# An eighth place for x in the column loop of a Hyena and MoE kernel, and three rooms instead of four for VectorE's weighted rows

## The chip, the cores and the metric

The kernel runs on one core of one Trainium2 chip. The metric is the device time of one execution in microseconds (us), as the median of several runs. Five engines work side by side: TensorE (PE, with its weight loads as PEld), VectorE (DVE), ScalarE (ACT), GpSimd (POOL) and SyncE (SP), whose queue starts nearly all DMA transfers here, strictly in the order in which the program issues them.

## What is computed

For four batches of 12608 positions by 128 channels, a long convolution along the positions (done with Fourier-like transforms), then a routing step: in each batch the 128 positions with the highest score go through a small two-layer network.

```python
h_filt = (np.maximum(pos_emb @ w1, 0.0) @ w2) * np.exp(-0.01 * pos)[:, None]
u = x * v
y = irfft(rfft(u, n=2*S, axis=1) * rfft(h_filt, n=2*S, axis=0), n=2*S, axis=1)[:, :S]
x = x * y                                   # input of the routing step
scores = x @ w_gate                         # per batch
top = argpartition(-scores[b], 128)[:128]
out = x;  out[b, top] += sigmoid(scores[top]) * (relu(x[top] @ moe_w1) @ moe_w2)
```

## The kernel before

**Tiles.** A batch is 32 channel tiles (`NG`), each of four channels; the main loop runs over 128 tiles t. A tile passes a forward transform (`f_s1`, L435, and `dft`, L278), a product with the filter's spectrum on VectorE (`f_v`, `f_u`, `f_m`, `f_y`), a fold on GpSimd (`f_sd`, L462 and L463), and three tiles later an inverse transform (`f_i`, L273, whose result ACT copies out at L486 and L487).

**The seam.** After the last tile of a batch (t = 34, 66, 98, and at the end) the main loop stops and `P1.run` does the *column loop* of that batch. Tile 35 of the first batch boundary, or its like, comes right behind it. In what follows "seam" is the end of one of the first three column loops together with the next few tiles.

**The column loop.** 128 columns of the output are made in 16 blocks of eight, each in two halves of four columns, so 32 halves h = 0 to 31. The blocks run in the order `ORD`; here they are numbered 0 to 15 in that order, and halves 2i and 2i+1 belong to block i. For each half TensorE makes the columns in a PSUM tile (`mm`, L552 and L556; a ring of four PSUM tiles); VectorE multiplies them in place into the block's x (`fin`, L567); VectorE, or GpSimd for the halves called far, multiplies by the gate weights into a *room* (`weigh`, L601); ACT sums each of the four columns of that room (`sums`, L611). The sums of the last four halves are put off into the following tiles ("late"). GpSimd also prepares columns (`comb`, L539).

**x and the stores.** Each block of x is loaded from DRAM into a *place* of 105 partitions by 1024 elements (`load_a`, L529, 420 KB), multiplied in place, and stored from there (L590, 420 KB). "Load i" and "store i" are those of block i. There are seven places: five buffers `xa` and two more, `XE`, that lie over buffers of the main loop (`qs` and part of `mt`; `ws` and part of `yz`), free while the column loop runs. Block i uses place i mod 7. The first five blocks are loaded in halves during tiles `LA` of the batch, ten tiles with one half each; loads 5 and 6, into `XE`, are issued when the column loop begins; when block i (from 1 on) is done, the program issues store i and then load i+6, whose place is that of block i-1. So on SP's queue load i+6 waits for store i-1 to land, and all later stores stand behind it. By this rule load 15 is issued after store 9, and the last users of the two `XE` places are blocks 12 and 13.

**What waits for the `XE` places.** The first is the copy of tile 35's transform into `qs` (L281, on ACT), right after the column loop. Behind it on ACT stand the two copies L437 of `f_s1`, seven late sums L611 and the copies L486 and L487 of `f_i`'s result; the third `f_i` after the loop needs the PSUM tile that those two empty. VectorE's next instruction, L444, needs the `qs` copy too.

**Rooms.** Halves that are not far and come before h = 28 take the four rooms `self.wx` in turn: two in the arena buffer `wx`, one in a `te` buffer and one in an `ht` buffer (in the last loop in `sd`). Late halves 30 and 31 use the buffer `wx` too.

**PSUM.** `bank2[k]` are three PSUM tiles of two banks (2 x 512 elements). In the column loop `bank2[1]` holds only the gate weights and, permanently, a mask in its *gap*: columns 364 to 428 of both banks (`gap`). The gap of `bank2[0]` holds scratch data of the top-128 search, which runs in the background of the next batch's tiles.

Of the kernel before, what the change touches and what calls it, by code (L numbers as in the profile page):

```python
# [11 lines left out]
AF = mybir.ActivationFunctionType  # L12
# [5 lines left out]
B, S, D, FO = 4, 12608, 128, 64  # L18
# [5 lines left out]
NG = 32  # L24
HC = 4 * N1
# [4 lines left out]
HB = 4  # L30
# [10 lines left out]
PJ = (N3 + 1) // 2  # L41
NC, CO = 4, 2
NE = 3
LA = range(32 - 12, 32 - 2)
NS, ND = 66, 4
NWARM = 8
JB = 9
# [6 lines left out]
OFF, _o = {}, 0  # L54
# [4 lines left out]
ARENA = _o  # L59
XE = [OFF["qs"][0] + k * 12 * D for k in range(2)]  # L60
CE = [o + 8 * D for o in XE]
POS0, HID0 = 0, PJ * N1


# [107 lines left out]
def hyena_moe(ctx, tc, xg, x2, pos, bw, ww, wg, mw1, mw2, fo, fc, c1, gx, cf, ci, wm, tk, out):  # L172
# [32 lines left out]
        return view(bank2[k], 0, shape)  # L205

    def gap(k, n):
        return bank2[k].rearrange("p (c x) -> p c x", c=2)[:, :, HC:HC + n]

    def c3(a):  # L210
        return a.rearrange("p (c x) -> p c x", c=2)
# [299 lines left out]
    class P1:  # L511
# [10 lines left out]
        def load_a(self, i, a=0, z=8):  # L522
            if i < len(ORD):
                k = ORD[i]
                j0, j1 = blocks[k]
                z = min(z, j1 - j0)
                o = i % (NX + len(XE))
                self.xa[k] = buf("xa", o, [128, 8, D]) if o < NX else view(arena, XE[o - NX], [128, 8, D])
                nc.sync.dma_start(self.xa[k][P0:P0 + PR, a:z], x2[self.b, :, j0 + a:j0 + z])  # L529

        def comb(self):
# [27 lines left out]
        def fin(self, h):  # L559
# [8 lines left out]
            if not end:  # L568
                self.weigh()
                far = ja >= JM and h + 1 < len(self.hbs) and h not in DW  # L570
                if h >= NL and not self.last:
                    o = OFF["cm"][0] + 2 * NC * D if h < 30 else OFF["wx"][0]
                    wx = view(arena, o + h % 2 * HB * D, [128, HB, D])
                elif far:
                    wx = view(arena, CE[self.pw % 2], [128, HB, D])
                    self.pw += 1
                else:
                    wx = view(arena, self.wx[self.nw % 4], [128, HB, D])
                    self.nw += 1
                self.mul = xa[:, js], wx[:, :n], ja, n, far, h  # L580
                if far:
                    self.weigh()
            else:
                for k in range(n):
                    nc.vector.scalar_tensor_tensor(out=junk, in0=xa[:, ja % 8 + k], scalar=1.0,
                                                   in1=self.wg, op0=ALU.mult, op1=ALU.mult,
                                                   accum_out=self.sc[:, ja + k:ja + k + 1])
            if ja + n == blocks[blk][1]:
                j0, j1 = blocks[blk]
                nc.sync.dma_start(out[self.b, :, j0:j1], xa[P0:P0 + PR, :j1 - j0])  # L590
                i = ORD.index(blk)
                if i:
                    self.load_a(i - 1 + NX + len(XE))
                if blk in CB:
                    self.comb()

# [20 lines left out]
        def run(self, ex):  # L617
            self.last = ex is not None
            self.ring = (0, 1, 2) if ex else (3, 2, 0, 1)
            self.wx = [OFF["wx"][0], OFF["wx"][0] + HB * D, OFF["te"][0] + (2 * HC if ex else 0),  # L620
                       OFF["sd"][0] if ex else OFF["ht"][0] + ((self.b + 1) * NG + 2) % NH * 2 * HC]
            self.wg = ps2(1, [128, D], f"wg_{self.b}")
            nc.scalar.copy(out=self.wg, in_=wgb)
            for k in range(len(XE)):
                self.load_a(NX + k)
            for k in range(2):
                self.comb()
            for h in range(len(self.hbs)):
# [416 lines left out]
    for t in range(NT + LAG):  # L1045
# [4 lines left out]
        if t < NT:  # L1050
# [9 lines left out]
            spare[0] = None  # L1060
            bg.hook("w", 1)
            load_u(t + NU)
            for k in range(2 * t, min(2 * t + 2, NX)):
                nc.scalar.activation(out=buf("xa", k, [128, 8 * D]), in_=one.to_broadcast([128, 8 * D]), func=AF.Copy,
                                     scale=0.0)
            if t == 2:
                nc.scalar.copy(out=negp, in_=c3(negm))
# [99 lines left out]
```

## Time and profile before

| | us |
|---|---|
| median of 3 runs | 873.44 (872.21 to 873.76) |
| the profiled execution | 867.68 |
| its span, first to last instruction | 865.9 |
| busy in the span: PE, DVE, POOL, ACT | 824.5 (95%), 762.4 (88%), 721.7 (83%), 614.0 (71%) |

The profile is of one execution, which was 5.76 us below the median of the runs. Busy shares are means over stages that are limited by different things, so the column loops and the seams are looked at by themselves. The column loops of the profiled execution run on TensorE from 254.5 to 291.4, 432.2 to 469.6, 610.9 to 647.9 and 780.6 to 818 us. TensorE's granted clock is 1.00 of full speed in all of them.

### The profile page before, as it was taken

To read this page: it belongs to the slowest core of one execution; us is meant where nothing else is said; L and a number is where in the kernel's file an instruction comes from. 1 tells how busy PE (TensorE), PEld (TensorE's weight loads), DVE (VectorE), ACT (ScalarE), POOL (GpSimd) and SP (SyncE) were. 2 spreads that over 40 slices of the span, in tenths; PEclk is the share of its full clock that TensorE was granted. 3 is DMA by queue.
4 is the path that set the end of the run, shared out by engine and by line. 5 is a ranking of instruction groups with operands and counts; after the bars stand their busy time and mean duration, and the time that the engine had idled before them with its cause. 6 is when DMAs were issued, how large, how long until landed. Compare 5 with 4: busy or idle time off the path is not lost.

```text
span 865.9 us, 45810 instructions
## 1 busy us (share of the span) xinstructions
PE 824.5 (95%) x19322; PEld 692.2 (80%) x19322; DVE 762.4 (88%) x1543; ACT 614.0 (71%) x2243; POOL 721.7 (83%) x837
## 2 busy tenths in 40 slices
PE   8899989999999999999999999999999999999965
PEld 5666668999999877777898677778997777779854
DVE  8989889999999789999996998999978989997883
ACT  7656565555549879895578898965797989657910
POOL 6899659999999689898997898989987989879610
PEclk9999999999999999999999999999999999999997
DMA  8044587777878877678778876788798767857910
GB/s 255 3 174 175 188 286 240 218 214 234 273 220 281 293 227 218 206 240 250 237 245 282 264 216 205 230 250 253 235 286 288 217 195 235 247 148 219 300 34 7
DMA packets 83134, 190.25 MB, mean 220 GB/s; under 512 B 9683, under 2 KB 46524, under 8 KB 82928
## 3 DMA queue, kind: packets, MB, share of 16 engines
q1 hardware_dynamic: 82672, 186.79, 68.2%
q8 instruction: 152, 2.49, 1.2%
q0 software_dynamic: 256, 0.52, 0.2%
q14 instruction: 54, 0.44, 0.2%
HBM read 147.57 MB, written 39.71 MB: 216 GB/s over the span
## 4 chain that ended last, share of the span: by engine, by line
PE 58%; DVE 21%; DMA 8%; ACT 6%; POOL 3%; issue 3%; POOLq 0%; SPq 0%; DVEq 0%; ACTq 0%
PE c L273 18%; PE c L278 13%; PE a L435 13%; DMA out_dram<-arena 4%; ACT arena L611 4%; DVE arena L449 2%; DVE c L450 2%; DVE big L361 2%; PE a L556 2%; PE a L552 2%; PE c L411 2%; DVE c L441 2%; DMA hd<-arena 2%; PE c L556 2%; DMA arena<-in_x_dram 1%
## 5 line engine op out<-in xcount | busy, mean ns | idle before, releaser
L273 PE MATMUL c<-ci_sb,arena 128*23 128x128 f32 x8128 | 253.1, 273 | 5.7 <-issue 2.2
L273 PEld LDWEIGHTS c<-ci_sb,arena 128*23 128x23 f32 x8128 | 231.0, 103 | 14.8 <-issue 6.6
L278 PE MATMUL c<-arena,cf_sb 128*32 128x364 f32 x2048 | 186.2, 470 | 6.0 <-ACT c L767 1.5
L435 PE MATMUL a<-cons,arena 128*32 128x182 f32 (+1 forms) x4096 | 187.9, 318 | 0.5 <-DVE arena L567 0.4
L435 PEld LDWEIGHTS a<-cons,arena 128*32 128x32 f32 (+1 forms) x4096 | 144.7, 110 | 37.0 <-issue 9.7
L486 ACT COPY big<-c 128x800 f32<-128x800 f32 x127 | 103.8, 817 | 81.6 <-PE c L273 81.1
L611 ACT ACTIVATE arena<-arena 128x128 f32<-128x128 f32 x504 | 148.0, 297 | 10.3 <-DVE arena L601 9.8
L462 POOL TENSOR_TENSOR arena<-arena 128x364 f32<-128x364 f32 x127 | 114.0, 898 | 47.4 <-DVE arena L456 36.7
L437 ACT COPY arena<-a 128x364 f32<-128x364 f32 x256 | 119.5, 467 | 41.9 <-PE a L435 37.0
L259 POOL TENSOR_TENSOR arena<-arena 128x508 f32<-128x508 f32 x128 | 139.2, 1088 | 10.3 <-DMA arena<-in_xg_dram 10.2
L449 DVE TENSOR_TENSOR arena<-c,arena 128x728 f32<-128x728 f32 x127 | 116.2, 915 | 3.8
L450 DVE TENSOR_TENSOR c<-c,arena 128x728 f32<-128x728 f32 x127 | 116.0, 914 | 0.0
L278 PEld LDWEIGHTS c<-arena,cf_sb 128*32 128x32 f32 x2048 | 79.4, 110 | 44.5 <-issue 30.0
L463 POOL TENSOR_TENSOR arena<-arena 128x364 f32<-128x364 f32 x127 | 114.4, 900 | 0.0
L611 ACT ACTIVATION_READ_ACCUMULATOR arena<-arena 128x1 f32 x504 | 95.2, 189 | 0.0
L444 DVE TENSOR_TENSOR c<-c,arena 128x364 f32<-128x364 f32 x128 | 69.5, 543 | 20.3 <-ACT arena L281 18.3
L506 POOL TENSOR_TENSOR big<-big,arena 128x224 f32<-128x224 f32 x128 | 74.4, 581 | 10.0
L539 POOL TENSOR_TENSOR arena<-big 128x512 f32<-128x512 f32 x64 | 79.9, 1280 | 0.6 <-PE a L552 0.3
L455 DVE TENSOR_TENSOR arena<-c,arena 128x364 f32<-128x364 f32 x127 | 68.2, 537 | 13.2 <-POOL big L505 0.5
L281 ACT COPY arena<-c 128x364 f32<-128x364 f32 x128 | 59.2, 462 | 23.1 <-DMA out_dram<-arena 7.1
L505 POOL TENSOR_TENSOR big<-big,arena 128x224 f32<-128x224 f32 x128 | 74.7, 584 | 0.0
L441 DVE TENSOR_TENSOR c<-c,arena 128x364 f32<-128x364 f32 x128 | 69.6, 544 | 2.6
(207 smaller groups left out, 1359.6 us busy)
## 6 DMA issues: line engine op xcount, KB each, us to landing
arena<-in_xg_dram SPq DMA_DIRECT2D x256, 254.0 KB, 3.5
arena<-hd SPq DMA_DIRECT2D x128, 364.0 KB, 4.1
out_dram<-arena SPq DMA_DIRECT2D x64, 420.0 KB, 5.7
arena<-in_x_dram SPq DMA_DIRECT2D x44, 420.0 KB, 5.0
hd<-arena SPq DMA_DIRECT2D x32, 364.0 KB, 2.8
arena<-in_x_dram SPq DMA_DIRECT2D x40, 210.0 KB, 4.4
arena<-in_pos_dram SPq DMA_DIRECT2D x16, 182.0 KB, 4.3
arena<-in_moe_w_dram SPq DMA_DIRECT2D x2, 512.0 KB, 4.7
```

Of the source, the lines that this page charges most:

```text
L259: nc.gpsimd.tensor_tensor(out=x, in0=x, in1=v, op=ALU.mult)
L273: nc.tensor.matmul(o[32 * k:32 * k + c.stop - c.start], lhsT=lhsT[:, c], rhs=rhs, start=True, stop=True)
L278: nc.tensor.matmul(pq[w][a:a + 32], lhsT=cf_sb[:, 2 * w + a // NQ, a % NQ:a % NQ + 32], rhs=te[:, a // NQ], start=True, stop=True)
L435: nc.tensor.matmul(tps[s // 2][c, s % 2], lhsT=u[:, s, c], rhs=c1_sb[:, k], start=True, stop=True)
L437: nc.scalar.copy(out=te[:, :, 2 * h:2 * h + 2].rearrange("p e s i -> p s e i"), in_=tps[h])
L441: nc.vector.tensor_tensor(out=nat(pq[:, 0]), in0=nat(pq[:, 0]), in1=rev(qs), op=ALU.add)
L449: nc.vector.tensor_tensor(out=mt, in0=uv, in1=ht[:, 0].unsqueeze(1).to_broadcast([128, 2, HC]), op=ALU.mult)
L450: nc.vector.tensor_tensor(out=uv, in0=uv, in1=ht[:, 1].unsqueeze(1).to_broadcast([128, 2, HC]), op=ALU.mult)
L462: eng.tensor_tensor(out=nat(sd[:, 0]), in0=nat(yz[:, 0]), in1=rev(yz[:, 1]), op=ALU.add)
L463: eng.tensor_tensor(out=nat(sd[:, 1]), in0=rev(yz[:, 0]), in1=nat(yz[:, 1]), op=ALU.subtract)
L486: nc.scalar.copy(out=ay[:, t % NG, :NJ + JM, ss], in_=o3[:, :, :NJ + JM].rearrange("p s x -> p x s"))
L611: nc.scalar.activation(out=x, in_=x, func=AF.Copy, accum_out=self.sc[:, j:j + 1])
```

## The change

Six places are now filled before the column loop instead of five: the arena buffer `wx` (two rooms before) becomes a place of 1024 elements, the first in the list `XP`. `XP` has eight places, `wx`, the five `xa`, the two `XE`, and block i uses place i mod 8. `LA` starts two tiles earlier and has twelve half loads; loads 6 and 7 are issued at the start of the loop; when block i is done, load i+7 follows store i, again into the place of block i-1. The last users of the `XE` places are therefore blocks 14 and 15. The zero fill of the places on ACT in the first tiles gets one more buffer, and tile 2 has two fills instead of one.

VectorE's weighted rows have three rooms in turn: the `te` buffer, the second bank of `bank2[1]` in PSUM, and the `ht` (or `sd`) buffer. To free that bank, `gap` puts both parts side by side into the first bank (columns 364 to 492).

```diff
-LA = range(32 - 12, 32 - 2)
+LA = range(32 - 14, 32 - 2)
+XP = [OFF["wx"][0], *(OFF["xa"][0] + k * 8 * D for k in range(NX)), *XE]
+NP0 = NX + 1
     def gap(k, n):
-        return bank2[k].rearrange("p (c x) -> p c x", c=2)[:, :, HC:HC + n]
+        return bank2[k][:, HC:HC + 2 * n].rearrange("p (c x) -> p c x", c=2)
-                o = i % (NX + len(XE))
-                self.xa[k] = buf("xa", o, [128, 8, D]) if o < NX else view(arena, XE[o - NX], [128, 8, D])
+                self.xa[k] = view(arena, XP[i % len(XP)], [128, 8, D])
-                    wx = view(arena, self.wx[self.nw % 4], [128, HB, D])
+                    wx = self.wx[self.nw % 3]
-                    self.load_a(i - 1 + NX + len(XE))
+                    self.load_a(i - 1 + len(XP))
-            self.wx = [OFF["wx"][0], OFF["wx"][0] + HB * D, OFF["te"][0] + (2 * HC if ex else 0),
-                       OFF["sd"][0] if ex else OFF["ht"][0] + ((self.b + 1) * NG + 2) % NH * 2 * HC]
+            o = OFF["te"][0] + (2 * HC if ex else 0), OFF["sd"][0] if ex else OFF["ht"][0] + ((self.b + 1) * NG + 2) % NH * 2 * HC
+            self.wx = [view(arena, o[0], [128, HB, D]), view(bank2[1], 512, [128, HB, D]), view(arena, o[1], [128, HB, D])]
             for k in range(len(XE)):
-                self.load_a(NX + k)
+                self.load_a(NP0 + k)
-            for k in range(2 * t, min(2 * t + 2, NX)):
-                nc.scalar.activation(out=buf("xa", k, [128, 8 * D]), in_=one.to_broadcast([128, 8 * D]), func=AF.Copy,
+            for k in range(2 * t, min(2 * t + 2, NP0)):
+                nc.scalar.activation(out=view(arena, XP[k], [128, 8 * D]), in_=one.to_broadcast([128, 8 * D]), func=AF.Copy,
                                      scale=0.0)
```

## Rows read from the trace of the kernel before

**Rows 1.** Busy time in the first and last column loop: start:end, length, engines, clock, DMA.
```profile
254.50:291.40 36.90, 36.90 (x674) 36.66 (x672) 31.86 (x52) 32.42 (x218) 34.52 (x31) 1.00 0.81 249
780.60:818.00 37.40, 37.36 (x675) 36.95 (x675) 30.68 (x55) 32.53 (x220) 33.48 (x31) 1.00 0.81 251
```

**Rows 2.** Who waited for whom, whole span: us in total, times, longest us.
```profile
DVE arena L567 <- DMA arena<-in_x_dram: 8.3, 6, 2.6
...
ACT arena L281 <- DMA out_dram<-arena: 7.1, 3, 2.7
```

**Rows 3.** TensorE in order of time, first seam: start, length, instructions, wait before them.
```profile
291.40 1.95 PE L273 MATMUL c<-ci_sb,arena 128*23 128x128 f32 x64
...
301.70 1.95 PE L273 MATMUL c<-ci_sb,arena 128*23 128x128 f32 x64 [0.42 <-ACT arena L487]
...
307.97 1.51 PE L273 MATMUL c<-ci_sb,arena 128*23 128x128 f32 x48 [1.40 <-issue]
...
316.39 1.93 PE L273 MATMUL c<-ci_sb,arena 128*23 128x128 f32 x64
...
320.62 1.60 PE L273 MATMUL c<-ci_sb,arena 128*23 128x128 f32 x52
```

**Rows 4.** TensorE in order of time, second and third seam.
```profile
470.90 1.95 PE L273 MATMUL c<-ci_sb,arena 128*23 128x128 f32 x64 [1.10 <-DVE arena L567]
...
480.94 1.95 PE L273 MATMUL c<-ci_sb,arena 128*23 128x128 f32 x64 [0.43 <-ACT arena L487]
...
647.85 1.95 PE L273 MATMUL c<-ci_sb,arena 128*23 128x128 f32 x64
...
657.29 1.95 PE L273 MATMUL c<-ci_sb,arena 128*23 128x128 f32 x64 [0.43 <-ACT arena L487]
```

**Rows 5.** The chain that ended last, first seam: start, length; load 14, store 12.
```profile
284.98 5.59 DMA arena<-in_x_dram
...
290.81 6.32 DMA out_dram<-arena
```

**Rows 6.** The same chain in the second and third seam: store 12 of each.
```profile
469.07 7.30 DMA out_dram<-arena
...
645.31 7.40 DMA out_dram<-arena
```

**Rows 7.** SP's issue of store 10, first seam, and its time from issue to landing.
```profile
L590 SPq DMA_DIRECT2D out_dram<-arena x1: 408/408/408, 289.9 to 289.9; - x1
...
DMA to landing us min/median/max: 5.1/5.1/5.1
```

**Rows 8.** The same of load 14, then of store 10, second seam.
```profile
L529 SPq DMA_DIRECT2D arena<-in_x_dram x1: 336/336/336, 465.5 to 465.5; - x1
...
DMA to landing us min/median/max: 4.5/4.5/4.5
...
L590 SPq DMA_DIRECT2D out_dram<-arena x1: 435/435/435, 468.1 to 468.1; - x1
...
DMA to landing us min/median/max: 5.7/5.7/5.7
```

**Rows 9.** The same of load 14, then of store 10, third seam.
```profile
L529 SPq DMA_DIRECT2D arena<-in_x_dram x1: 336/336/336, 641.3 to 641.3; - x1
...
DMA to landing us min/median/max: 5.2/5.2/5.2
...
L590 SPq DMA_DIRECT2D out_dram<-arena x1: 417/417/417, 644.4 to 644.4; - x1
...
DMA to landing us min/median/max: 5.8/5.8/5.8
```

**Rows 10.** First column loop: ACT's last sum of half 18, VectorE's weighing of half 21.
```profile
281.77 0.29 ACT L611 ACTIVATE arena<-arena 128x128 f32<-128x128 f32 x1
...
282.89 0.68 DVE L601 TENSOR_TENSOR arena<-arena,c 128x512 f32<-128x512 f32 x1
```

**Rows 11.** ACT in tile 2: the zero fill of one place.
```profile
120.27 1.06 ACT L1064 ACTIVATE arena<-cons 128x1024 f32<-128x1024 f32 x1
```

## The prediction

> **What bounds the kernel now.** I first looked at the column loops, which the change is about, in the view of busy time by stretch [rows 1]. TensorE is busy for all 36.90 us of the first loop and 37.36 of 37.40 us of the last, at clock 1.00; VectorE has 31 to 32 us of work there and ACT 32. So TensorE sets the loop's length, and nothing that VectorE or ACT saves inside it shortens it. Then the view of waits [rows 2]: VectorE waits 8.3 us in all, six times, for loads of x. This is what an eighth place acts on. The same view holds a second DMA wait, 7.1 us in three pieces: the copy into `qs` behind each of the first three loops waits for a store. Third, TensorE in order of time [rows 3, 4]. A tile costs it 4.23 us in the steady state (316.39 to 320.62). From the first `f_i` behind the loop to the third, two tiles, it takes 10.30 us in the first seam (291.40 to 301.70), 11.14 in the second (480.94 less 470.90, and the 1.10 us that it waited before), and 9.44 in the third, where two steady tiles are 8.46. The third `f_i` waits last for L487 on ACT. Fourth, the chain that ended last names what holds ACT: store 12, issued at 290.81, landing 6.32 us later at 297.13 [rows 5], then at 476.37 and 652.71 [rows 6]. From these landings to the third `f_i` it is 4.57, 4.57 and 4.58 us [rows 3, 4]: the same ACT work each time. So a seam ends by the landing of the store that frees the first `XE` place, plus 4.57 us. TensorE loses 1.84, 2.68 and 0.98 us there, 5.5 us in all; this is the most that a better landing can give back.
>
> **Loads of x: what goes.** Load 15 now follows store 8 on SP, not store 9, so it takes the moment at which load 14 was issued before: 284.98, 465.5 and 641.3 [rows 5, 8, 9]. Each block has its x one step earlier, and I expect all of VectorE's 8.3 us to go. I cost this at nothing: TensorE is the bound while the loop runs, and behind the loop VectorE's next instruction, L444, needs the `qs` copy, which is late anyway. What is late next is that copy. Only in the second loop did a load wait reach TensorE, as 1.10 us before its first `f_i` [rows 4]; it too lies ahead of the 476.37 landing, so it is hidden by the copy.
>
> **The store that frees the `XE` place: what is added.** The last block in the first `XE` place was 12 and is 14. So the `qs` copy now waits for store 14. Behind it on ACT stand the copies of `f_s1`, seven late sums and `f_i`'s copies; VectorE's L444 and TensorE's third `f_i` wait for these. When does store 14 land? SP's transfers land here in the order of issue, close one behind the other once several are under way. Store 10 to store 12 took, from issue plus time to landing: first seam 289.9 + 5.1 = 295.0 to 297.13, 1.06 us per store [rows 5, 7]; second 468.1 + 5.7 = 473.8 to 476.37, 1.27 [rows 6, 8]; third 644.4 + 5.8 = 650.2 to 652.71, 1.25 [rows 6, 9]. Load 15 now lands where load 14 did: 290.57, 470.0 and 646.5 [rows 5, 8, 9]. Behind it come stores 9 to 14, six of them, with nothing between. Before, there were five transfers between load 14 and store 12 (store 9, load 15, stores 10 to 12). So store 14 lands at
>
> - first seam: 290.57 + 6 x 1.06 = 296.93, which is 0.2 us earlier than 297.13;
> - second: 470.0 + 6 x 1.27 = 477.62, 1.25 us later than 476.37;
> - third: 646.5 + 6 x 1.25 = 654.0, 1.3 us later than 652.71.
>
> Sum: +2.3 us. The first seam gains a little because load 15 was issued late there and left the queue a hole. The bounds of this term: at 1.06 us per store everywhere it is -0.2 + 0.0 + 0.2, or zero; at 1.27 everywhere it is 1.06 + 1.25 + 1.4, or +3.7 us. I take each seam's own spacing, since it is measured in the very stretch. The data of store 14 is there in time: TensorE makes 32 halves in 36.9 us, 1.15 each [rows 1], so half 29 is done 2.3 us before the first `f_i` and multiplied some 0.7 us later, at about 289.8, 468.2 and 646.2, and the store waits only for its turn.
>
> Store 15 now frees the second `XE` place, where block 13 was last. VectorE's L455 of the next tile writes there. Between the `qs` copy and it stand L444, L441, L449 and L450, with 364, 364, 728 and 728 elements; at the 0.68 us for 512 of [rows 10] an estimate for these is 2.9 us, while store 15 lands one spacing, 1.3 us, behind store 14. Hidden by 1.6 us; nothing. Without that cover it would cost up to 1.3 us a seam.
>
> **The two tiles earlier start of `LA`** moves a load out of each loop onto SP's queue among the tiles' own loads. TensorE was not seen waiting for a load there, and the place `wx` has been idle since the late sums. Nothing, at worst a fraction of a us per batch.
>
> **Three rooms.** Six of the 17 room halves of a loop go to PSUM; the instructions are the same in number and size. The third room back must be free: VectorE's weighing of half 21 began at 282.89 and ACT's last sum of half 18, with 0.29 us from 281.77, was done at 282.06 [rows 10]. So the tightest case has 0.8 us to spare, and no wait comes. No row has ACT reading 128 columns from PSUM with an accumulated sum; between a little faster and a little slower than 0.29 us per column I take it as equal. Below nothing there is no gain, since TensorE is the bound; above, see the rivals.
>
> **Zero fill.** Tile 2 has one more fill of 1.06 us on ACT [rows 11]. ACT is the lighter engine of the first tiles, as `f_i` and its copies have hardly begun. Between 0 and 1.06; I take 0.
>
> **The stall in the first seam**, 1.40 us before a part of the fourth `f_i` [rows 3], has no releaser in the trace and no like in the other seams. I leave it; if the quieter queue removes it, -1.4.
>
> Sum: +2.3 us on the profiled execution, 867.7 to 870.0. That execution was 5.76 us under the median of the runs, and I put the same difference on the median: 873.44 + 2.3 = 875.7.
>
> **Rivals.**
>
> *No change.* The queue is denser than before, since nothing holds stores 9 to 13 back behind a waiting load, and store 14 lands when store 12 did. This is the lower bound of the term, the first seam's 1.06 us for each store. For it: that seam, and that a load among stores may cost more than a store. Against: the other two seams. Time: 873.4.
>
> *Faster.* Store 14 is not held by those ahead of it. Issued at 289.8, 468.2 and 646.2 and landing after the shortest time in the rows for a store, 5.1 us [rows 7], it would land at 294.9, 473.3 and 651.3, early by 2.2, 3.1 and 1.4. This is more than TensorE lost in each seam, so all 5.5 us come back: 867.9, and 866.5 if the stall goes too. Half of it would give 870.7. It decides as soon as store 14 lands more than 0.6 us earlier than store 12 did, seam for seam. Against it stands that store 12 itself took 6.32 to 7.40 us where store 10 took 5.1 to 5.8 [rows 5 to 9]: those behind land later. The Trainium skill (DMA: Bandwidth & Descriptors, section "Two DMAs through the same engine are not ordered") says that the descriptors of one queue start in order but are pipelined, and that nothing orders transfers across the DMA engines. By that rule a late store could overtake, and this rival would hold; the landings in the rows rise evenly and show no overtaking.
>
> *Rooms bind.* If ACT's sums from PSUM took 0.1 us more per column, the 24 columns of a loop would cost ACT 2.4 us. That is 0.8 of spare and then 1.6 us of waiting by VectorE, at worst passed on to TensorE through the ring in each of four loops: 6.4 us, 879.8. From about 0.03 us per column on it would begin to show. Nothing in the rows speaks for slower sums.
>
> *It does not do what it says.* The load waits stay. Then load 15 was not moved a step ahead, and the time would be that of the first two cases; I give this nothing of its own.
>
> **How the numbers follow.** A measurement of this kernel tells about 0.2%, 1.75 us, from no change. The forecast case (store 14 behind its queue, zero to +3.7 us, with a fill or the stall beside it): 0.58; of this I count 0.37 beyond +1.75 and 0.21 within. No change: 0.20, of which 0.03 below -1.75. Faster, -2 to -7 us: 0.16, 0.15 of it beyond the limit. Rooms: 0.06, slower. So faster 0.18, same 0.39, slower 0.43. The range from 869.5 to 879 leaves out the better part of the faster rival, some 0.08, and the worst of the rooms and of the queue, some 0.08. The likeliest case alone has 873 to 877.5.
>
> **What would show it.** Right: no wait of L567 for loads of x; load 15 issued behind store 8; the `qs` copy waiting for store 14, in the second and third seam longer than before; the third `f_i` 4.57 us behind that landing. Wrong: the copy waiting for dft on TensorE instead of a store, or store 14 landing well before 476 and 652 when the stretches before are laid side by side; then the faster rival holds. VectorE's L601 waiting for ACT's L611 would show the rooms. The forecast is wrong as a whole if the third `f_i` behind a loop is not set by the `qs` copy any more.

## The result, and the profile after

| | before | after |
|---|---|---|
| median of 9 runs each, us | 873.76 (871.97 to 877.88) | 883.05 (877.21 to 885.81) |
| ratio to before, 95% interval | | 1.0112 (1.0084 to 1.0140) |
| the profiled execution, its span | 867.68, 865.9 | 883.05, 881.2 |

The change makes the kernel 9.3 us slower, where 2.3 us were forecast. In the code after, most lines have moved by one or two: L567 is now L568, L601 is L602, L611 is L612, L281 is L283, L487 is L489 and L273 is L275.

The first and the last column loop of after, in the view of busy time by stretch (start:end, length, then PE, PEld, DVE, ACT and POOL, clock, DMA share, GB/s), answer [rows 1]:

```profile
258.58:298.62 40.04, 37.27 (x677) 36.62 (x673) 31.79 (x52) 32.74 (x209) 34.03 (x31) 1.00 0.82 266
...
790.10:831.60 41.50, 38.19 (x675) 36.87 (x675) 30.20 (x55) 33.74 (x218) 33.43 (x31) 1.00 0.79 249
```

The loop was 36.9 us and TensorE was busy in all of it. Now it is 40.04 us, and TensorE stands still for 2.77 of them. No engine has much more work than before: VectorE's is the same and ACT's grew by 0.3 us. So it is waiting, and the view of waits, whole span, tells where (us in total, times, longest us), beside [rows 2]:

```profile
DVE arena L602 <- ACT c L612: 31.5, 23, 2.5
...
POOL arena L602 <- DVE arena L568: 19.8, 14, 2.0
...
ACT arena L612 <- DVE arena L602: 18.5, 16, 4.9
...
ACT arena L283 <- DMA out_dram<-arena: 3.3, 2, 2.1
```

VectorE's load waits, 8.3 us before, are gone. In their place VectorE waits 31.5 us in 23 pieces, six per loop and five in the last, for ACT's sums from PSUM (tile `c`). GpSimd and ACT then wait for VectorE. In order of time, VectorE and ACT of the first loop (start, length, instruction, wait before it):

```profile
264.27 0.69 DVE L602 TENSOR_TENSOR c<-arena,c 128x512 f32<-128x512 f32 x1
264.86 0.68 DVE L568 TENSOR_TENSOR arena<-a,arena 128x512 f32<-128x512 f32 x1
266.64 0.69 DVE L602 TENSOR_TENSOR arena<-arena,c 128x512 f32<-128x512 f32 x1 [1.10 <-ACT c L612]
...
274.92 0.69 DVE L602 TENSOR_TENSOR c<-arena,c 128x512 f32<-128x512 f32 x1
...
278.68 0.69 DVE L602 TENSOR_TENSOR arena<-arena,c 128x512 f32<-128x512 f32 x1 [2.49 <-ACT c L612]
...
264.38 0.29 ACT L612 ACTIVATE arena<-arena 128x128 f32<-128x128 f32 x1
264.67 0.29 ACT L612 ACTIVATE arena<-arena 128x128 f32<-128x128 f32 x1
265.05 0.26 ACT L612 ACTIVATE c<-c 128x128 f32<-128x128 f32 x1
265.44 0.26 ACT L612 ACTIVATE c<-c 128x128 f32<-128x128 f32 x1
265.84 0.26 ACT L612 ACTIVATE c<-c 128x128 f32<-128x128 f32 x1
266.24 0.26 ACT L612 ACTIVATE c<-c 128x128 f32<-128x128 f32 x1
...
267.37 0.31 ACT L612 ACTIVATE arena<-arena 128x128 f32<-128x128 f32 x1 [0.75 <-DVE arena L602]
...
277.07 0.26 ACT L612 ACTIVATE c<-c 128x128 f32<-128x128 f32 x1
...
278.28 0.26 ACT L612 ACTIVATE c<-c 128x128 f32<-128x128 f32 x1
```

Three things are to be seen. First, the weighing at 266.64 writes to a room in the arena that nobody has used yet, the third in turn, and still it begins only when ACT has done the four sums of the PSUM room weighed before it. The wait is not for a room. Second, ACT's sums from PSUM are shorter by themselves (0.26 against 0.29 us) but start 0.40 us apart, where those from SBUF start 0.29 apart. Third, the wait can be longer than four sums. The room of 274.92 was written by 275.61, but ACT, which takes its sums in order, still had sums of other rooms to do and began with this one at 277.07; the next weighing waited for all of it, 2.49 us. Of the six waits in this loop, 8.5 us in all, the two longest, 2.49 and 2.48 us, reach TensorE through the ring of PSUM tiles. TensorE's own view has a wait behind each, and these make up the 2.77 us:

```profile
280.03 1.09 PE L553 MATMUL c<-big,cons 128*64 128x128 f32 x16 [1.14 <-DVE arena L568]
...
293.23 1.09 PE L553 MATMUL a<-big,cons 128*64 128x128 f32 x16 [1.63 <-DVE arena L568]
```

The seams of after, TensorE's first and third `f_i` of each and the `qs` copy on ACT, answer [rows 3, 4]:

```profile
298.62 1.95 PE L275 MATMUL c<-ci_sb,arena 128*23 128x128 f32 x64
...
307.04 1.93 PE L275 MATMUL c<-ci_sb,arena 128*23 128x128 f32 x64
...
476.42 1.94 PE L275 MATMUL c<-ci_sb,arena 128*23 128x128 f32 x64
...
486.59 0.63 PE L275 MATMUL c<-ci_sb,arena 128*23 128x128 f32 x16 [0.42 <-ACT arena L489]
...
482.12 0.46 ACT L283 COPY arena<-c 128x364 f32<-128x364 f32 x1 [2.15 <-DMA out_dram<-arena]
```

In the first seam the two tiles now take 8.42 us and lose nothing (10.30 before); the second still ends 4.47 us behind the start of a `qs` copy that waited for a store. With longer loops the stores have more time to land.

The whole result can be added up from TensorE's order of time. The table has, for each kernel, the four loops and then the three stretches from the start of a loop to the third `f_i` behind it (TensorE's first matmul of the loop to that of the `f_i`; the fourth loop from its first matmul, 780.64 in before and 790.24 in after, to the end of its last). The sum is that of the three stretches and the fourth loop, less the same of before. All but the first two rows are experiments below.

| kernel | loops 1 to 4, us | to the third `f_i` | sum | measured |
|---|---|---|---|---|
| before | 36.87, 38.70, 36.84, 37.53 | 47.17, 48.74, 46.28 | | |
| after | 40.04, 40.03, 40.03, 41.34 | 48.46, 50.20, 49.20 | +9.5 | +9.8 |
| rooms alone | 40.05, 40.03, 40.03, 41.33 | 48.47, 49.11, 48.46 | +7.7 | +6.8 |
| places alone | 36.83, 36.83, 36.83, 37.53 | 47.03, 49.35, 49.21 | +3.4 | +5.0 |
| row in another tile | 43.50, 43.51, 43.49, 51.93 | 52.48, 52.50, 52.47 | +29.7 | +28.9 |
| slow sums alone | 37.26, 37.27, 37.72, 38.65 | 48.88, 47.17, 50.85 | +5.8 | +4.9 |
| before, reordered | 36.96, 38.37, 37.43, 37.53 | 46.80, 46.79, 45.85 | -2.8 | -3.1 |
| places reordered, again | 36.83, 36.83, 36.84, 37.53 | 45.26, 46.66, 46.02 | -4.3 | -5.4 |

"Measured" is the ratio less one, times the median of before in the same comparison. Each row is one execution, "measured" a comparison of medians. In these rows the two agree within 2 us, so loops and seams hold nearly all of the difference. In two runs that are not in the table they do not: with the row read from SBUF the sum is +14.1 against +17.1 measured, and in the first run of the places reordered -5.8 against -3.1. The rest of the 15.3 us between the two spans lies elsewhere, 4.05 us of it ahead of the first loop, which starts at 258.58 instead of 254.53. That start scatters: the last kernel of the table starts its first loop at 254.47 in one execution and at 258.66 in another, and three kernels with seven places at 254.53, 256.87 and 257.41. One piece of the change can be seen there all the same, the second zero fill of tile 2. VectorE and TensorE of after, shortly behind it:

```profile
125.75 0.55 DVE L446 TENSOR_TENSOR c<-c,arena 128x364 f32<-128x364 f32 x1 [1.66 <-ACT c L1068]
...
129.88 1.43 PE L280 MATMUL c<-arena,cf_sb 128*32 128x364 f32 x16 [0.86 <-DVE arena L458]
```

ACT's copy L1068 stands behind the two fills, VectorE waits for that copy (0.71 us in before), and TensorE then for VectorE. TensorE has this wait, of 0.85 to 0.87 us, in all eleven runs with eight places and in none of the three with seven.

### The profile page after: what moved, and what is told of

Read it like the earlier page. It is cut to its first block, busy times and chain, and to the rows that moved or that the text cites. A ratio compares the mean times of both kernels' runs of the same rounds, so it can differ in the third digit from the quotient of the medians.

```text
span 881.2 us, 45824 instructions
## 1 busy us (share of the span) xinstructions
PE 829.2 (94%) x19322; PEld 683.0 (78%) x19322; DVE 760.3 (86%) x1543; ACT 620.3 (70%) x2244; POOL 721.0 (82%) x837
## 3 DMA queue, kind: packets, MB, share of 16 engines
q8 instruction: 152, 2.49, 1.1%
## 4 chain that ended last, share of the span: by engine, by line
PE 53%; DVE 22%; ACT 15%; DMA 4%; issue 4%; POOL 1%; POOLq 0%; DVEq 0%; ACTq 0%
PE c L275 19%; PE c L280 14%; PE a L437 13%; ACT arena L612 10%; ACT c L612 3%; DMA hd<-arena 2%; DVE arena L451 2%; DVE c L452 2%; DVE big L363 2%; DVE c L443 2%; DVE arena L421 2%; DVE c L446 1%; DMA out_dram<-arena 1%; DVE arena L457 1%; DVE arena L458 1%
## 5 line engine op out<-in xcount | busy, mean ns | idle before, releaser
L275 PE MATMUL c<-ci_sb,arena 128*23 128x128 f32 x8128 | 249.1, 273 | 3.1 <-issue 1.5
L275 PEld LDWEIGHTS c<-ci_sb,arena 128*23 128x23 f32 x8128 | 227.9, 103 | 11.0 <-issue 4.4
L280 PE MATMUL c<-arena,cf_sb 128*32 128x364 f32 x2048 | 182.5, 470 | 7.1 <-ACT arena L439 2.2
L437 PE MATMUL a<-cons,arena 128*32 128x182 f32 (+1 forms) x4096 | 184.0, 318 | 0.0
L437 PEld LDWEIGHTS a<-cons,arena 128*32 128x32 f32 (+1 forms) x4096 | 138.0, 110 | 42.8 <-issue 10.5
L612 ACT ACTIVATE arena<-arena 128x128 f32<-128x128 f32 x408 | 120.0, 297 | 18.5 <-DVE arena L602 18.5
L280 PEld LDWEIGHTS c<-arena,cf_sb 128*32 128x32 f32 x2048 | 68.9, 110 | 52.4 <-issue 30.1
L612 ACT ACTIVATION_READ_ACCUMULATOR arena<-arena 128x1 f32 x408 | 77.0, 189 | 0.0
L283 ACT COPY arena<-c 128x364 f32<-128x364 f32 x128 | 59.1, 462 | 21.5 <-PE c L280 8.0
```

The lines of the kernel that those rows point to most:

```text
L275: nc.tensor.matmul(o[32 * k:32 * k + c.stop - c.start], lhsT=lhsT[:, c], rhs=rhs, start=True, stop=True)
L280: nc.tensor.matmul(pq[w][a:a + 32], lhsT=cf_sb[:, 2 * w + a // NQ, a % NQ:a % NQ + 32], rhs=te[:, a // NQ], start=True, stop=True)
L437: nc.tensor.matmul(tps[s // 2][c, s % 2], lhsT=u[:, s, c], rhs=c1_sb[:, k], start=True, stop=True)
L612: nc.scalar.activation(out=x, in_=x, func=AF.Copy, accum_out=self.sc[:, j:j + 1])
```

## The experiments

All ratios are to the kernel before on the same chip. Its median there was 869.88 to 871.73 us, not 873.76, so times, and the ranges expected for them, are to be compared by the ratio. The expectations name three theories. A: every weighing waits for ACT because row and room lie in one PSUM tile. B: the slower sums from PSUM hold the loop by themselves. C: the store that frees the `XE` place costs the time.

**The two parts of the change, each alone.** First the rooms without the eighth place: the kernel before with the edit of `gap` and three rooms in turn, the buffer `wx` unused.

```diff
-                    wx = view(arena, self.wx[self.nw % 4], [128, HB, D])
+                    wx = self.wx[self.nw % 3]
...
+            self.wx = [view(arena, o[0], [128, HB, D]), view(bank2[1], 512, [128, HB, D]), view(arena, o[1], [128, HB, D])]
```

> The kernel before with its seven places, and only the rooms of the change: te, second bank of the PSUM tile, ht; and the gap moved. Theories A and B: the whole loss is here, loops 39.5 to 40 us, time 881 to 886. Theory C: nothing or little, 873 to 876.

Measured: 876.8 us, ratio 1.0078 (1.0053 to 1.0102); VectorE waits for ACT 31.6 us in 23 pieces, as in after. The loops are as theories A and B expected, but the loss is not all here: 6.8 us of 9.8, less than their range. Then the places without the PSUM room: the kernel after with two rooms in turn, both in SBUF.

```diff
-                    wx = self.wx[self.nw % 3]
+                    wx = self.wx[self.nw % 2]
-            self.wx = [view(arena, o[0], [128, HB, D]), view(bank2[1], 512, [128, HB, D]), view(arena, o[1], [128, HB, D])]
+            self.wx = [view(arena, k, [128, HB, D]) for k in o]
```

> The changed kernel with eight places, but only two rooms in turn, te and ht, and none in PSUM. Theories A and B: no loss from sums; VectorE may wait 0.3 us at a time for the second room back; loops 36.9 to 37.5 us. What is left is the store that frees the first XE place, which I put at +2.3 us: 873 to 877. Theory C: 881 to 885.

Measured: 875.42 us, ratio 1.0057 (1.0031 to 1.0083). The time lies in the expected range only because before was faster on this chip: the loss is 5.0 us, where +2.3 was expected. The first three loops are 36.83 us, with no PSUM room and one load wait of 0.7 us, which TensorE does not see; the wait of the `qs` copy for a store grew from 7.1 us [rows 2] to 11.3. ACT's view of the three copies:

```profile
300.29 0.46 ACT L283 COPY arena<-c 128x364 f32<-128x364 f32 x1 [2.64 <-DMA out_dram<-arena]
...
478.51 0.46 ACT L283 COPY arena<-c 128x364 f32<-128x364 f32 x1 [3.89 <-DMA out_dram<-arena]
...
657.80 0.46 ACT L283 COPY arena<-c 128x364 f32<-128x364 f32 x1 [4.81 <-DMA out_dram<-arena]
```

So both parts cost time, the rooms in the loops, the places behind them. Together they cost less than the sum, since a loop that ends later leaves the store less to be waited for (3.3 us in after). Even two rooms are enough for VectorE: its waits for a room there are 3.2 us in four pieces, and the loops show none of it.

**Which access is it?** The weighing on VectorE reads the gate weights' row from a copy in the first bank of `bank2[1]`, the tile whose second bank is the new room. With the row read from its original in SBUF no weighing of an SBUF room touches that tile.

```diff
-                eng, w = (nc.gpsimd, wgb) if far else (nc.vector, self.wg)
+                eng, w = (nc.gpsimd, wgb) if far else (nc.vector, wgb)
```

> The changed kernel, but VectorE's weighing takes the gate weights from their SBUF tile wgb instead of the copy in PSUM, which lies in the first bank of the same PSUM tile as the new room. Theory A (shared tile: every weighing that follows a PSUM room waits until ACT has written all four sums there, since weights and room are one tile): VectorE's waits for ACT fall from 31.5 us to under 4, the column loops from 40.0 to about 37 us, the time to 872 to 877. ACT still needs 0.40 us per PSUM column. Theory B (slow sums from PSUM with three rooms bind by themselves): the waits stay above 15 us, loops at 39 or more, time 879 to 884. Theory C (the store that frees the XE place costs the time): loops unchanged, 881 to 885.

Measured: 888.1 us, ratio 1.0197 (1.0164 to 1.0230), which none of the three theories gave. Of theory A the first part came nearly true: VectorE's waits for ACT fell from 31.5 to 4.7 us, and the weighing behind the first PSUM room began at 266.36, before ACT's last sum of that room at 267.07. So the wait goes with the tile. The time rose for another reason, seen in the groups by line (busy, mean ns of one | idle before):

```profile
L602 POOL TENSOR_TENSOR arena<-arena,wgb 128x512 f32<-128x512 f32 x47 | 65.0, 1400 | 4.2 <-DVE arena L568 2.5 <-ACT arena L612 1.6
L602 DVE TENSOR_TENSOR arena<-arena,wgb 128x512 f32<-128x512 f32 x55 | 54.9, 998 | 4.8 <-ACT arena L612 4.7
L602 DVE TENSOR_TENSOR c<-arena,wgb 128x512 f32<-128x512 f32 x24 | 25.9, 1078 | 0.0
```

In after the same groups took 1094, 681 and 685 ns: with both inputs in SBUF, VectorE's weighing and GpSimd's hold each other up. The Trainium skill says so (SBUF — State Buffer, section "SBUF: two separate sides"): the two engines share a pair of ports, and whichever starts first keeps the other out for a whole instruction when VectorE has two inputs in SBUF and GpSimd reads SBUF. The groups agree, and single weighings here took from 0.68 to 1.71 us. It is also what the copy of the row in PSUM saves.

Then the other access: ACT's sums of the PSUM room write their by-product to a row in SBUF, so ACT only reads that tile.

```diff
-                nc.scalar.activation(out=x, in_=x, func=AF.Copy, accum_out=self.sc[:, j:j + 1])
+                nc.scalar.activation(out=o, in_=x, func=AF.Copy, accum_out=self.sc[:, j:j + 1])
```

> The changed kernel, but ACT writes the by-product of the PSUM room's sums to a scratch of 128 elements in SBUF instead of back into PSUM. Theory A: with no ACT write into the tile of the weights no weighing waits, loops about 37 us, time 872 to 877. Theory B: depends on the cadence alone: if a PSUM column then takes 0.29 us like an SBUF column, 873 to 877; if it stays at 0.40, 879 to 884 with VectorE's waits still there. Theory C: 881 to 885 whatever the cadence.

Measured: 879.64 us, ratio 1.0103 (1.0069 to 1.0137). The waits stayed (30.8 us in 23 pieces), and so did the distance of the sums, on ACT in order of time:

```profile
264.02 0.28 ACT L616 ACTIVATE arena<-c 128x128 f32<-128x128 f32 x1
...
264.42 0.28 ACT L616 ACTIVATE arena<-c 128x128 f32<-128x128 f32 x1
```

The distance says nothing about PSUM here: all these by-products go to one row, and that alone makes each sum wait for the one before, as an experiment below shows. The waits of VectorE do say something. Two engines that both only read the tile, in different banks, still go one behind the other. The instruction lists of the kernel after say why. Each line is an instruction of the first loop with the engines whose semaphores it waits for; VectorE's first, then ACT's:

```
L602 TENSOR_TENSOR c1<-arena,c1      [waits DVE]
L568 TENSOR_TENSOR arena<-a1,arena   [waits DMA, PE]
L602 TENSOR_TENSOR arena<-arena,c1   [waits DVE, Activation]

L612 ACTIVATE arena,sc<-arena        [waits DVE]
L612 ACTIVATE arena,sc<-arena x3
L612 ACTIVATE c1,sc<-c1              [waits DVE, Activation]
L612 ACTIVATE c1,sc<-c1 x3           [waits Activation]
```

The waits are in the program. Accesses to a PSUM tile stand in order there whatever banks they touch and, as the last run shows, also where both only read, even two of ACT itself; for the arena it does so only where elements overlap. The Trainium skill asks for less (PSUM — Partial Sum Buffer, section "PSUM bank collisions raise a hardware error"): two different engines have to be kept apart in one bank and the same 32 partitions, not in two banks. No run here lets two engines into a PSUM tile at once, so whether it would go well is not shown.

**The row in another tile.** If that is so, the row may go to the second bank of `c0`, of which the ring uses the first.

```diff
-            self.wg = ps2(1, [128, D], f"wg_{self.b}")
+            self.wg = view(bank2[0], 512, [128, D])
```

> The kernel after, with one edit: the copy of the gate weights lies in the second bank of tile c0 (which the ring uses only in its first bank) instead of the first bank of the tile whose second bank is the new room. Theory: VectorE's waits for ACT come from two things in one PSUM tile, the row it reads and the room that ACT sums; apart, the waits fall from 57 us in all (31.5, 23 and 2.5 of one group and what follows) to under 6, the loops fall from 40.0 to about 37.3 us, and the time falls to about that of the places alone, 875 us (872.5 to 877.5). The sums from PSUM keep starts 0.40 us apart, 2.6 us of ACT per loop, which then lie beside other work. Rival: the slower sums alone hold the loop; then the waits become waits for a room and the time stays at 879 to 884.

Measured: 900.25 us, ratio 1.0331 (1.0265 to 1.0397). (The 57 us in the expectation are a slip: 31.5 us is already the total, 23 the number of waits and 2.5 us the longest.) One part of this expectation came true: no weighing waits for ACT's PSUM sums any more. The time was wrong by 25 us, and by the theory's own rule. The wait moved to TensorE, whose halves in `c0` now wait for the last weighing that read the row there:

```profile
264.26 1.09 PE L557 MATMUL c<-big,cons 128*64 128x128 f32 x16 [0.84 <-DVE arena L602]
...
275.38 1.09 PE L553 MATMUL c<-big,cons 128*64 128x128 f32 x16 [1.74 <-DVE arena L602]
...
281.78 1.09 PE L553 MATMUL c<-big,cons 128*64 128x128 f32 x16 [1.81 <-DVE c L602]
```

The wait follows the row from tile to tile. In the first three loops there is no tile in which the row and a room could lie without company, so a version of the change free of this wait was not found. The same row move together with the reordered places (below):

> The kernel after with both edits: the gate weights' row in the second bank of c0, and the two places over the transform's buffers used as fourth and fifth. Theory: both causes gone, waits of VectorE for ACT under 6 us, waits of the qs copy for a store under 2, time 866 to 871, below the kernel before (873.8). Rival: the sums from PSUM or the queue hold it at 873 or more.

Measured: 901.19 us, ratio 1.0330 (1.0263 to 1.0397), for the same reason. The other half of the theory held: the copy into `qs` waits for no store.

**Is it PSUM that makes the sums slow, or the wait for the one before?** The kernel of the places alone, without a PSUM room, with the by-products of all sums of VectorE's rooms in one row of SBUF. The program then makes each wait for the one before.

```diff
+                self.out = [self.scr] * n
...
-                nc.scalar.activation(out=x, in_=x, func=AF.Copy, accum_out=self.sc[:, j:j + 1])
+                nc.scalar.activation(out=o, in_=x, func=AF.Copy, accum_out=self.sc[:, j:j + 1])
```

> The kernel with eight places and two rooms in SBUF, none in PSUM, with one edit: the sums of VectorE's rooms write their by-product to one row of 128 elements, so that in the program each sum waits for the sum before it, as the sums from PSUM do in the kernel after. Nothing reads PSUM here. Theory: the wait for the predecessor sets the 0.40 us between starts; then these sums from SBUF also start 0.39 to 0.41 us apart where they are back to back, and the loop becomes ACT's, at 17 halves x 4 columns x 0.11 = 7.5 us more of ACT per loop, time 885 to 900. Rival: reading PSUM sets it; then they start 0.29 us apart as before and the time is that of the places alone, 875 us.

Measured: 895.7 us, ratio 1.0266 (1.0185 to 1.0347). On ACT, sums from SBUF, 0.43 to 0.44 us apart, a little more than expected:

```profile
264.46 0.31 ACT L616 ACTIVATE arena<-arena 128x128 f32<-128x128 f32 x1 [1.52 <-DVE arena L605]
...
264.90 0.31 ACT L616 ACTIVATE arena<-arena 128x128 f32<-128x128 f32 x1
...
265.33 0.31 ACT L616 ACTIVATE arena<-arena 128x128 f32<-128x128 f32 x1
```

And the opposite: the PSUM room's columns alternate between two tiles, so that each sum waits only for the sum before the last.

```diff
-view(bank2[1], 512, [128, HB, D])
+[view(bank2[k], 512, [128, 2, D]) for k in (1, 0)]
```

> The kernel after with the PSUM room spread over two PSUM tiles, its four columns alternating between the second banks of c1 and c0, and the gate weights' row in the second bank of c2. Each sum then waits in the program for the sum before the last, not for the last. One look at ACT alone. Theory (the wait for the predecessor sets the 0.40 us): back to back these sums start 0.26 to 0.30 us apart though they read PSUM. Rival (reading PSUM sets it): 0.40 as in after. The kernel as a whole is slower than after, 890 to 920 us, since the ring's halves in c0 and c2 then wait for the room and for the row as they did for the row in c0.

Measured: 946.6 us in one run, worse than expected, as the ring's halves wait for two strangers in their tiles. For ACT's sums alone, in order of time:

```profile
268.50 0.26 ACT L620 ACTIVATE c<-c 128x128 f32<-128x128 f32 x1
...
268.79 0.26 ACT L620 ACTIVATE c<-c 128x128 f32<-128x128 f32 x1
...
269.07 0.26 ACT L620 ACTIVATE c<-c 128x128 f32<-128x128 f32 x1
```

They read PSUM and start 0.28 us apart. So PSUM is not slow for these sums; the wait for the predecessor is what costs the 0.11 us.

**How much is slow sums, how much the shared tile?** Again the places alone, with only every third of VectorE's halves, six per loop, summed in line (the edit above with `self.out` set where `self.nw % 3 == 1`).

> The kernel with eight places and two rooms in SBUF, none in PSUM, with one edit: of VectorE's halves every third, the six per loop that lie in PSUM in the kernel after, has its sums write their by-product to one row, so that these 24 sums per loop wait for the one before (0.435 us from start to start in the trace where all sums did this). So ACT pays 24 x 0.14 = 3.4 us per loop, somewhat more than for PSUM (2.6), and no weighing reads a tile that ACT is summing. Theory (the shared tile, not the slower sums, makes the loop long): ACT's spare time takes most of it, the first loop has 36.8 to 38 us, time 875 to 879. Rival (the slower sums make it): the first loop has 39.5 to 41 us as in the kernel after, time 884 to 890.

Measured: 875.85 us, ratio 1.0056 (1.0028 to 1.0084). The first and the fourth loop by stretch:

```profile
257.88:295.14 37.26, 37.16 (x676) 36.61 (x673) 32.84 (x54) 32.29 (x205) 34.08 (x31) 1.00 0.79 256
788.05:826.70 38.65, 37.75 (x675) 36.93 (x675) 30.45 (x54) 33.21 (x212) 33.45 (x31) 1.00 0.80 259
```

Over the places alone the four loops grew by 0.43, 0.44, 0.89 and 1.12 us, 2.9 in all; in after they are longer by 3.21, 3.20, 3.20 and 3.81, 13.4 in all. These slow sums cost ACT more than those of after (0.435 against 0.40 us). In measured time slow sums alone cost nothing that can be told (ratio 1.0056, and 1.0057 for the places alone). So the slow sums alone make at most 22% of the longer loops, and the wait for the shared tile, alone or with them, is left to make the rest. How the two add with three rooms instead of two was not tried.

**The store behind the loop.** The eight places in another order: the two `XE` places as fourth and fifth, with two rooms in SBUF. Blocks 3, 4, 11 and 12 use them, loads 3 and 4 are issued when the loop begins, and stores 11 and 12 free them.

```diff
-XP = [OFF["wx"][0], *(OFF["xa"][0] + k * 8 * D for k in range(NX)), *XE]
+XP = [OFF["wx"][0], *(OFF["xa"][0] + k * 8 * D for k in range(2)), *XE, *(OFF["xa"][0] + k * 8 * D for k in range(2, NX))]
+LK = (0, 1, 2, 5, 6, 7)
-                self.load_a(NP0 + k)
+                self.load_a(3 + k)
-            ph[b].load_a(k, e * HB, (e + 1) * HB)
+            ph[b].load_a(LK[k], e * HB, (e + 1) * HB)
```

> The kernel with eight places and two rooms in SBUF, none in PSUM, with one edit: the two places over the transform's buffers are used as fourth and fifth instead of seventh and eighth, so blocks 3, 4, 11 and 12 lie in them, and stores 11 and 12 free them instead of 14 and 15. Theory: the copy into qs behind a loop waits for the store that frees the first of these places; with store 11 that wait falls from 11.3 us (three pieces) to under 2, and the time from 875.4 to 867 to 871. Rival 1: the copy then waits for TensorE or VectorE at nearly the same moment, and the time stays within 2 us of 875. Rival 2: loads 3 and 4, issued only at the loop's start, come late, VectorE waits for them for over 1 us a loop, and what the seam gives the loop takes.

Measured: 868.62 us, ratio 0.9965 (0.9932 to 0.9998). Again, in more rounds, beside the seven places of before in the same manner (`XE` as fourth and fifth, four rooms in SBUF):

> The same kernel as the eight places reordered, beside the seven places reordered on one chip and in more rounds. Theory: ratio to before 0.9965 as before, within 0.994 to 0.999, and 0 to 2 us under the seven places reordered, which is what the eighth place is worth by itself, through the load wait of one loop. Rival: no difference to before, then the gain seen was the chip's.

> The kernel before, with one edit: of its seven places the two over the transform's buffers are used as fourth and fifth instead of sixth and seventh, so blocks 3, 4, 10 and 11 lie in them and stores 10 and 11 free them instead of 12 and 13. No eighth place, four rooms in SBUF. Theory (the order of places, not their number, sets the seams): the qs copy's 7.1 us of waiting for a store falls below 2, the seams give back 3 to 4 us as in the eight places reordered, and the load waits of VectorE (8.3 us) stay but lie under TensorE's work except the 1.9 us that they cost in one loop; time 868 to 872 where before has 871.7 to 873.8, ratio 0.995 to 0.999. Rival (the eighth place is what makes room in the queue): the load waits grow, and the ratio is 1.00 or above.

Measured: eight places 863.99 us, ratio 0.9938 (0.9916 to 0.9961), a little beyond the range expected, and 2.5 us under the seven, where 0 to 2 were expected; seven places 866.47 us, ratio 0.9964 (0.9942 to 0.9986). The first seam of the eight, TensorE in order of time, then the wait of the copy, now L284; then the two DMA waits of the seven:

```profile
291.30 1.94 PE L276 MATMUL c<-ci_sb,arena 128*23 128x128 f32 x64
295.52 1.93 PE L276 MATMUL c<-ci_sb,arena 128*23 128x128 f32 x64
299.73 0.51 PE L276 MATMUL c<-ci_sb,arena 128*23 128x128 f32 x12
```

```profile
ACT arena L284 <- DMA out_dram<-arena: 2.3, 1, 2.3
```

```profile
DVE arena L568 <- DMA arena<-in_x_dram: 12.0, 9, 3.3
...
ACT arena L283 <- DMA out_dram<-arena: 1.1, 1, 1.1
```

The order of the places gives back the seam's loss, with seven as with eight. The eighth place takes the load waits away as well (with seven they grew from 8.3 to 12.0 us, in nine pieces, as the rival had it, though its ratio did not come; TensorE saw 1.46 us of them before its first `f_i` in the second seam, 0.53 in the third and 1.01 behind its first `f_i` in the first). The two ratios differ by 0.0026 and their intervals overlap, so what the eighth place adds by itself is likely but not shown. The eight places in this order, with two rooms in SBUF, have the lowest time here, clearly below before and after.

## Why the prediction was wrong

**Three rooms: this step failed.** It compared ACT's last sum with the next use of the same room, found 0.8 us to spare, concluded "no wait comes", and put the term at nothing; the rooms alone cost 6.8 us. The comparison holds for the room: in after VectorE waits for no room in SBUF. But the weighing needs more than a room. The row of weighing in [rows 10] reads `arena<-arena,c`: the `c` is the gate weights' row, in the very tile that the change turns into a room. With that, the weighing behind a PSUM room stands behind four sums of ACT and behind what ACT has to sum before them, the longest time 2.5 us; VectorE waits 31.5 us in all, and the first loop grows by 3.17 us. The other claim of the step, on 0.29 us for sums from PSUM ("I take it as equal"), was wrong too: 0.40.

**The rival "rooms bind"** had the sign, a part of the mechanism (0.1 us per column; 0.11 measured) and the row that would show it (VectorE's weighing waiting for ACT). Its price of 6.4 us is near the 7.7 that the rooms alone cost, but by the wrong sum, as slow sums by themselves are worth 2.9 us at most. It got a chance of 0.06 because "nothing in the rows speaks for slower sums"; the row just named spoke for a wait. The range ended at 879.0 and left out the place where its 6.4 us and the store's 2.3 meet.

**Loads of x: right.** The load waits are gone in after, and in the places alone but for one of 0.7 us. Load 15 goes out behind store 8; SP's issues of the first loop in after, with six stores right behind that load, 9 to 14:

```profile
287.04 0.40 SPq L591 DMA_DIRECT2D out_dram<-arena  x1
288.90 0.34 SPq L530 DMA_DIRECT2D arena<-in_x_dram  x1
289.29 9.02 SPq L591 DMA_DIRECT2D out_dram<-arena  x6
```

One part needs a word: the load wait in the second loop of before, which was 1.87 us longer than that of the places alone, was called hidden by the copy. It was, as long as the copy came late. With the places reordered it may be a gain, but this is not shown: the second loop is 1.54 us shorter with eight places than with seven, its stretch to the third `f_i` 0.13 in one execution, where the copy waited 2.3 us for a store, and 1.33 in the other (45.46 us), where it waited 0.9.

**The store that frees the `XE` place: right in kind, a little small.** The places alone test it without the rooms. From the start of the loop, the copy behind store 14 began at 42.56, 43.80 and 44.74 us; the forecast landings, from the loops of before, are 42.40, 45.42 and 42.99. The two loops that miss are 1.6 us early and 1.75 late, and in the second the third `f_i` came 5.55 us behind the copy's start, not about 4.5. What was wrong is the spacing. By its issue and time to landing, load 15 landed 34.8, 37.2 and 36.6 us into the loop (forecast 36.0, 37.8 and 35.5), and the six stores behind it took 1.29, 1.10 and 1.36 us each (forecast 1.06, 1.27, which is 1.285 by the rows, and 1.25). So the spacing measured in a seam of before did not carry over, and the first seam came out right because two misses cancelled. Seam for seam the stretches changed by -0.14, +0.61 and +2.93 us, where -0.2, +1.25 and +1.3 were forecast. The term is +3.4 us in this execution against +2.3 forecast, within its bounds (0 to +3.7) in part by luck; the ratio says +5.0 (2.7 to 7.2). In after, the longer loops hid the first of these waits altogether: its third `f_i` is not set by the copy, which the prediction named as a sign that the forecast is wrong as a whole.

**Zero fill: too small.** It was taken at 0, within 0 to 1.06 us; TensorE waits 0.86 us for it, as shown above. **`LA`: nothing seen.** From the third `f_i` of a seam to the next loop TensorE takes 129.4, 129.8 and 124.6 us in after, 130.5, 130.1 and 123.4 in before; a fraction of a us could not be told. **The stall in the first seam** became 0.18 us in after. It was priced at up to -1.4; but stalls of its kind stand elsewhere in other executions (0.99 us at 654.75 in the places reordered, again), so that the change took it away is not shown.

**The sum.** Forecast: loops 0, seams +2.3. Seen in after: the loops 1 to 3 longer by 7.7 and the fourth by 3.8, of which the seams of the first three give back 2.0, as they are no longer gated as hard. That is +9.5; outside it lie the +0.9 of the fill and the -1.2 of the stall.

## What to carry to other kernels

Before a buffer is moved into a free bank of a PSUM tile, list who else touches any bank of that tile: a program that orders accesses by tile makes neighbours of two banks wait for each other, and the wait goes along when the neighbour is moved. A check that a buffer is free in time covers only one operand; go through all operands of the instruction. Where a copy waits for a store because of the place that the store frees, changing the order in which places are used can be worth more than adding a place.

## What was not expected of the hardware

ACT's sum of 128 elements from PSUM is no slower than from SBUF: 0.26 against 0.29 to 0.31 us for one, and 0.28 against 0.29 us from start to start where it does not wait for the sum just before. A wait of ACT for its own last instruction costs 0.11 us from PSUM (0.40) and 0.14 us from SBUF (0.43 to 0.44). Each sum is followed by a read of the accumulator, 0.18 to 0.19 us. A sum that need not wait begins while that read still runs (in after at 264.67, the read from 264.58 to 264.77); one that waits begins 0.03 us behind it (265.44, the read from 265.22 to 265.41). Where VectorE's 128 x 512 product has both inputs in SBUF while GpSimd runs the same, it takes 998 to 1078 ns in the mean instead of 681 to 685, and GpSimd's takes 1400 instead of 1094.
